# Attention and two feed-forward layers on one core: the first layer's up-projections from seven block products, and a fixed order for TensorE

## The chip, the cores and the metric
The kernel runs on one core of a Trainium2 chip. A core has TensorE (matmuls), VectorE, ScalarE and GpSimd, and SyncE (SP), whose queue starts nearly all transfers here. The metric is the device time of one execution in microseconds. Times of before and after come from several runs; durations of instructions come from one profiled execution each.

## The reference
```python
def phi(x):                                   # x: (4, 8, 576, 64), w_phi: (64, 128)
    proj = einsum('bhsd,df->bhsf', x, w_phi)
    proj = proj - max(abs(proj), axis=-1, keepdims=True)
    return concatenate([exp(proj), exp(-proj)], axis=-1)
q_p, k_p = phi(q), phi(k)
kv = einsum('bhsf,bhsd->bhfd', k_p, v);  z = sum(k_p, axis=2)
attn = einsum('bhsf,bhfd->bhsd', q_p, kv) / (einsum('bhsf,bhf->bhs', q_p, z)[..., None] + 1e-06)
x = attn.transpose(0, 2, 1, 3).reshape(2304, 512)
h = maximum(maximum(x @ w1, x @ w2), x @ w3)  # first layer, 512 -> 768
x = h @ w_out                                 # 768 -> 512
xn = x / sqrt(mean(x * x, -1) + 1e-06) * rms_g
g = xn @ w_gate                               # second layer, 512 -> 1536
out = (g / (1 + exp(-g)) * (xn @ w_val)) @ w_out2
```
All weights of the two layers are given as float64, all other inputs as float32.

## The kernel before
**Order.** The program collects operations in a `Planner`: each has an engine, a rank (its due time by hand-written formulas), an estimated duration, the buffers that it reads and writes and, on TensorE, a form ("rows": the array split in two by rows; "cols": split by columns; "whole"). `order` then places them one after the other by the estimated times, picks by rank among what could start within 0.11 us, gives every buffer a slot of its ring, and the program is written out in that order. So each engine's order is static, and a wait holds everything behind it on that engine. `SP` issues the loads, spills and fetches in one such order too.

**Attention.** Eight units (two heads of two batches each), each in three steps of 384 tokens. A step has, for TensorE, the projections of k (`k_proj`, L431, tile pk) and q (`q_proj`, L500, tile pq), the sums over tokens `kv_sum` (L464 and L461, tile pkv), `attend` (L531, tile nd) and `turn`, a transpose of the result (L551, tile pq). k_proj, q_proj and turn are in row form, kv_sum and attend in column form. Around them stand maxima, subtractions and exponentials on VectorE, ScalarE and GpSimd (an all-partition maximum for q). At the end of a step ScalarE rounds the transposed result (`x_round`, L559) and VectorE forms the remainder (`x_rest`, L562).

**Products in three parts.** Both operands of a matmul of the feed-forward layers are split into a rounded part and a remainder of TensorE's 32-bit format; a product is three matmuls, high x high, high x low, low x high (`mm3`, L386).

**Weights.** A weight tile of 512 columns is loaded in its double width (`wst`), and cut to single precision with five VectorE instructions (`narrow`, L657 to L671), then rounded by ScalarE (L679) and its remainder taken by GpSimd (L685, L687). The results go to 24 slots, `wp`.

**First layer.** For each of six blocks of 128 hidden features (m) and six tiles of 384 tokens (t): three up-projections of 12 matmuls each (`plan_up`, tiles first and up), their maximum (L871, L874), its split (L850, L851), and four down-projections of three matmuls (tile po), summed in `acc` by VectorE (L822). The first tiles of m = 0 (tile first) may run while attention ends.

**Second layer.** It works on token pairs (j) and pairs of hidden blocks already in seven block products instead of eight: `Duo` holds for one weight and a pair of tiles the sums "11", "12", "S1" to "S4", "22", `plan_forms` makes the matching block sums of the tokens, and `quad` issues for each weight the seven products of six matmuls into three accumulators (L1060, tiles ua and ub), from which ScalarE and VectorE (L1068, L1074, L1080, L1082) build the four results. Down-projections have 512 columns (tile pd). Token pairs 0 and 1 go through all six hidden pairs first; the weights are spilled to DRAM (`spill`) and come back (`fetch`) for token pair 2. The statistics for the norm (`plan_stats`, `plan_scale`) are taken at the end of the first layer.

## Time and profile before

| what | value |
|---|---|
| median of 3 runs | 868.77 us (867.83 to 869.34) |
| profiled execution | 867.84 us, its span 866.1 us |
| busy, share of the span | TensorE 98%, VectorE 75%, ScalarE 48%, GpSimd 26% |
| DMA | 98.68 MB, mean 114 GB/s |

The span goes from the first to the last instruction of the trace. A busy share is the union of an engine's instructions, each from its start to its end as the profiler records it; neighbouring instructions of one engine can overlap, so that their durations add to more than the time that they take. Ends of matmuls are modelled.

### The profile page before, as it was taken

Reading aid. Unit: us, or ns where it says so; the run is one execution under the profiler, and the core shown is the slowest. Engines: PE = TensorE matmul, PEld = TensorE weight load, DVE = VectorE, ACT = ScalarE, POOL = GpSimd, SP = SyncE. Lnnn points to the kernel's source line nnn. Section 1 sums busy time; section 2 is a strip of 40 time slices with the busy share of each in tenths; the row PEclk is TensorE's granted clock in tenths of the full one; section 3 lists DMA queues with packets and bytes.
Section 4 is the critical chain, followed back from the end, with each engine's and each line's share of the span. In section 5 each row is a group of like instructions: output and inputs, shape, how many; then the busy total and the mean of one; then the engine's idle time right before and its main releaser. Section 6 shows DMA issues by size and latency. Waiting matters only on the chain.

```text
span 866.1 us, 17038 instructions
## 1 busy us (share of the span) xinstructions
PE 853.0 (98%) x6784; PEld 801.3 (93%) x6784; DVE 650.8 (75%) x1301; ACT 413.0 (48%) x848; POOL 228.4 (26%) x157
## 2 busy tenths in 40 slices
PE   8999999999999999999998999999999999999997
PEld 7888889999999999999997999898989999999996
DVE  4899987888644986465998998998888867355445
ACT  5999994453211312124578755454535434432222
POOL 3555553454202311013244333322232200000000
PEclk9999999999999999999999999999999999999999
DMA  7444412132110123022012555544532213455551
GB/s 216 127 140 131 148 35 74 60 112 73 50 49 1 55 93 134 12 99 73 7 43 79 189 182 183 171 155 161 195 122 73 73 73 122 167 202 200 211 195 73
DMA packets 70686, 98.68 MB, mean 114 GB/s; under 512 B 5968, under 2 KB 42960, under 8 KB 70608
## 3 DMA queue, kind: packets, MB, share of 16 engines
q1 hardware_dynamic: 70528, 97.57, 33.7%
q8 instruction: 53, 0.87, 0.4%
q14 instruction: 25, 0.20, 0.1%
q10 hardware_dynamic: 80, 0.03, 0.0%
HBM read 69.27 MB, written 28.31 MB: 113 GB/s over the span
## 4 chain that ended last, share of the span: by engine, by line
PE 83%; DVE 9%; DMA 3%; ACT 3%; issue 1%; SPq 1%; POOL 0%; ACTq 0%; DVEq 0%
PE up L386 23%; PE pd L386 14%; PE ua L1060 13%; PE ub L1060 10%; PE po L386 8%; PE nd L531 4%; PE pkv L464 3%; DMA wst<-in_moe_w_gate_dram 2%; PE first L386 2%; PE pq L500 2%; PE pk L431 2%; DVE x L952 1%; DVE wm L671 1%; PE pq L551 1%; PE pkv L461 1%; DVE hl L851 1%
## 5 line engine op out<-in xcount | busy, mean ns | idle before, releaser
L386 PE MATMUL up<-x,wp 128*128 128x384 f32 x1188 | 216.9, 334 | 0.0
L386 PEld LDWEIGHTS up<-x,wp 128*128 128x128 f32 x1188 | 207.0, 188 | 0.0
L1060 PE MATMUL ua<-x,wp 128*128 128x384 f32 x720 | 142.0, 337 | 5.8 <-ACT sn L1068 2.4
L1060 PEld LDWEIGHTS ua<-x,wp 128*128 128x128 f32 x720 | 126.2, 188 | 10.9 <-ACT sn L1068 3.9
L386 PE MATMUL pd<-wp,hh 128*128 128x512 f32 x432 | 133.7, 390 | 0.0
L850 ACT CAST hh<-hf 128x384 fp32r<-128x384 f32 x108 | 55.1, 515 | 125.8 <-DVE hf L874 88.1
L1060 PE MATMUL ub<-x,wp 128*128 128x384 f32 x504 | 97.9, 335 | 0.3 <-DVE hf L1074 0.2
L386 PEld LDWEIGHTS pd<-wp,hh 128*128 128x128 f32 x432 | 80.6, 188 | 14.8
L685 POOL TENSOR_TENSOR wa<-wa,wp 128x512 f32<-128x512 f32 x32 | 45.0, 1405 | 177.2 <-ACT wp L679 121.7
L874 DVE TENSOR_TENSOR hf<-up,hf 128x384 f32<-128x384 f32 x66 | 36.7, 556 | 71.5 <-PE up L386 71.4
L1060 PEld LDWEIGHTS ub<-x,wp 128*128 128x128 f32 x504 | 88.4, 188 | 1.4 <-DVE hf L1074 0.5
L386 PE MATMUL po<-hh,wp 128*128 128x384 f32 x288 | 85.7, 337 | 0.2
L822 DVE TENSOR_TENSOR acc<-pd,acc 128x512 f32<-128x512 f32 x90 | 61.6, 687 | 32.3 <-PE pd L386 32.2
L386 PE MATMUL pd<-wp,hl 128*128 128x512 f32 x216 | 84.9, 393 | 0.0
L506 POOL PARTITION_ALL_REDUCE mq<-pc x24 | 66.5, 2779 | 56.6 <-ACT pc L503 51.4
L822 DVE TENSOR_TENSOR acc<-po,acc 128x384 f32<-128x384 f32 x120 | 64.4, 553 | 2.7 <-PE po L386 2.7
L851 DVE TENSOR_TENSOR hl<-hf,hh 128x384 fp32r<-128x384 f32 x108 | 62.8, 582 | 3.6 <-ACT hh L850 2.9
L1074 DVE TENSOR_TENSOR hf<-ub,hf 128x384 f32<-128x384 f32 x54 | 29.8, 553 | 42.0 <-ACT hf L1068 21.1
L650 ACT ACTIVATE wm<-wst 128x512 f32<-128x512 f32 x60 | 40.5, 675 | 39.3 <-DMA wst<-in_moe_w_gate_dram 16.3
L1068 ACT COPY sn<-ua 128x384 f32<-128x384 f32 x54 | 25.7, 477 | 65.4 <-PE ua L1060 65.3
L386 PEld LDWEIGHTS po<-hh,wp 128*128 128x128 f32 x288 | 53.0, 188 | 0.9 <-issue 0.4
L671 DVE SCALAR_TENSOR_TENSOR wm<-wst,wm 128x512 f32<-128x512 uint32 x60 | 49.8, 836 | 0.4
(102 smaller groups left out, 1448.4 us busy)
## 6 DMA issues: line engine op xcount, KB each, us to landing
wst<-in_moe_w_dram SPq DMA_DIRECT2D x18, 512.0 KB, 3.6
wst<-in_moe_w_out_dram SPq DMA_DIRECT2D x18, 512.0 KB, 3.6
wst<-in_moe_w_gate_dram SPq DMA_DIRECT2D x12, 512.0 KB, 4.1
wst<-in_moe_w_val_dram SPq DMA_DIRECT2D x12, 512.0 KB, 3.6
dwh<-wp SPq DMA_DIRECT2D x20, 256.0 KB, 2.8
wp<-dwh SPq DMA_DIRECT2D x20, 256.0 KB, 5.1
kraw<-in_kT_dram SPq DMA_DIRECT2D x24, 192.0 KB, 4.0
qraw<-in_qT_dram SPq DMA_DIRECT2D x24, 192.0 KB, 3.9
```

The lines of the kernel that those rows point to most:

```text
L386: mm(out=ps, lhsT=a, rhs=b, start=start and i == 0, stop=stop and i == n - 1)
L506: nc.gpsimd.partition_all_reduce(buf(f"mq{n}.{c}").rearrange("p a c -> p (a c)"), buf(f"pc{n}.{c}").rearrange("p a c -> p (a c)"), P, bass ...
L531: mm(out=nd[r, i, j * (D + 1):(j + 1) * (D + 1)], lhsT=e[:, j, q], rhs=kvs[:, u, b, :], start=u == 0, stop=u == 1)
L650: nc.scalar.activation(out=buf(f"wm{self.id}").bitcast(FP32), in_=self.view()[1].bitcast(FP32), func=ACTF.Abs)
L671: nc.vector.scalar_tensor_tensor(out=mf, in0=lo.bitcast(U32), scalar=2.0 ** -52, in1=mf, op0=ALU.mult, op1=ALU.mult)
L685: eng.tensor_tensor(out=a, in0=a, in1=r32(buf(self.h)), op=ALU.subtract)
L822: nc.vector.tensor_tensor(out=acc, in0=p, in1=acc, op=ALU.add)
L850: pl.op("ACT", rank, act_us(n), lambda: nc.scalar.copy(out=buf(h)[:, 0:n], in_=buf(f)[:, 0:n]), r=[f], w=[h])
L851: pl.op("DVE", rank + 0.6, dve_us(n), lambda: nc.vector.tensor_tensor(out=buf(l)[:, 0:n], in0=buf(f)[:, 0:n], in1=r32(buf(h)[:, 0:n]), op= ...
L874: pl.op("DVE", b_at(m, t, q), dve_us(n), lambda f=f, p=p, n=n: nc.vector.tensor_tensor(out=buf(f)[:, 0:n], in0=buf(p)[:, 0:n], in1=buf(f)[ ...
L1060: mm(out=buf(ps)[:, 0:TW], lhsT=x, rhs=y, start=start and n == 0, stop=stop and n == 3 * KH - 1, skip_group_check=True)
L1074: pl.op("DVE", q_at(i, q + off), dve_us(TW), lambda: nc.vector.tensor_tensor(out=buf(dst), in0=raw(), in1=buf(dst), op=ALU.add), r=[ps], w ...
```

## The change
The first layer gets the form of the second. Token pairs 0 and 1 go through all three pairs of hidden blocks (first pass), then token pair 2 (second pass); for each weight, `plan_chain` issues seven products of six matmuls. The new `Duo` of the first layer prepares pairs of weight tiles of w1, w2 and w3 (two of the nine pairs during attention, with VectorE taking their remainders), all weights of the first layer are spilled and come back for the second pass, and two hidden blocks share one accumulation of a down-projection. Attention's results are copied unsplit into `acc` (`x_out`, ScalarE); `plan_forms` makes the block sums of the tokens for both layers, each time with four differences and seven splits. The first chain has banks of its own ("fa", "fb") and may run while attention ends. In attention every operation of TensorE gets a place in one fixed line (`seq`): in each step attend of three steps ago and kv_sum (column form), then q_proj, k_proj of two steps ahead and turn (row form). The norm's statistics of token pairs 0 and 1 are planned into the second pass, and one pair of the second layer's weight tiles is prepared there ahead of its turn, spilled and fetched (`AHEAD`). Ring sizes, pools and many due times change with it.

```diff
+        line = sorted((o["seq"], o["i"]) for o in ops if o["seq"] is not None)
+        line = [i for _, i in line][::-1]
+
         def place(o):
-
...
+            if o["seq"] is not None and o["i"] != line[-1]:
+                return None
...
-    banks("up", (0, 1, 2, 3))
-    banks("first", (0, 1))
-    banks("po", (4, 5, 6, 7))
-    banks("pn", (7,))
+    banks("fa", (0,))
+    banks("fb", (1,))
     banks("ua", (0, 1))
     banks("ub", (2, 3, 4))
     banks("pd", (5, 6, 7))
+    banks("pn", (7,))
...
-    U = 17.65
-    LOAD = 0.4
+    U = 15.42
+    ORDER = (4, 5, 6)
+
+    def place_of(n, c, i):
+        return n * NCH + c, (ORDER.index(i) + 4 if i > 3 else i)
+
+    def at_step(n, c, i):
+        a, b = place_of(n, c, i)
+        return U / 3 * (a + 0.14 * b)
+
+    LEAD, QLEAD, TLAG = 2, 3, 0
...
-            pl.op("PE", rk - 9.34, KPROJ, lambda c=c: k_proj(c), r=["wphi", f"kraw{n}.{c}"], w=pk, form="rows")
+            pl.op("PE", at_step(n, c - LEAD, 5), KPROJ, lambda c=c: k_proj(c), r=["wphi", f"kraw{n}.{c}"], w=pk + ["klast"] * (n == NU - 1 and c == NCH - 1), form="rows", seq=place_of(n, c - LEAD, 5))
...
+                pl.op("PE", at_step(n, c, 2 + j), (NSUB + (c == 1)) * 2 * HALF, lambda c=c, j=j: kv_sum(c, j), form="cols", seq=place_of(n, c, 2 + j),
...
-        def x_round(c, h, t, a0, a1, b0, b1):
-            nc.scalar.copy(out=x_at("h", t, hp)[:, b0:b1], in_=buf(f"xt{n}.{c}.{h}")[:, a0:a1])
-
-        def x_rest(c, h, t, a0, a1, b0, b1):
-            nc.vector.tensor_tensor(
-                out=x_at("l", t, hp)[:, b0:b1], in0=buf(f"xt{n}.{c}.{h}")[:, a0:a1], in1=r32(x_at("h", t, hp)[:, b0:b1]),
-                op=ALU.subtract,
-            )
+        def x_out(c, h):
+            a = hp * TW + h * CH
+            dst, src = buf(f"raw{g * NCH + c}")[:, a:a + CH], buf(f"xt{n}.{c}.{h}")[:, 0:CH]
+            if XENG[h] == "ACT":
+                nc.scalar.copy(out=dst, in_=src)
+            else:
...
+            pl.op("PE", at_step(n, c + 3 - QLEAD, 4), 0.65, lambda c=c: q_proj(c), form="rows", r=["wphi", qr], w=pq, seq=place_of(n, c + 3 - QLEAD, 4))
...
+                pl.op("PE", at_step(n, c + 3, j), 6 * HALF, lambda c=c, j=j: attend(c, j), form="cols", seq=place_of(n, c + 3, j),
...
+            pl.op("PE", at_step(n, c + 3 + TLAG, 6), 0.16, lambda c=c: turn(c), form="rows", r=["ident", xs], w=xt, seq=place_of(n, c + 3 + TLAG, 6))
+            for h in range(2):
+                raw = new(f"acc{g * NCH + c}", f"raw{g * NCH + c}")
+                pl.op(XENG[h], rk + 5.37, act_us(CH, True) if XENG[h] == "ACT" else dve_us(CH), lambda c=c, h=h: x_out(c, h), r=[xt[h]], w=[f"{raw}:{hp}.{h}"])
...
-            eng = nc.vector if self.id < 4 else nc.gpsimd
+            eng = nc.gpsimd
...
+            e = self.early
+            last, gate = [] if e else ["mqlast"], [] if e == 2 else ["kdone"]
+            veng = "DVE" if e else VENG
+            reng = ["DVE"] * 4 if e else RENG
...
+    VENG = "DVE"
+    RENG = ["POOL", "POOL", "POOL", "DVE"]
+    duos1 = [[Duo(w, m, max(0, 2 - i) if m == 0 else 0) for i, w in enumerate((w1, w2, w3))] for m in range(NM1)]
+    rows1 = [[rows(wo1, 2 * m + z) for z in range(2)] for m in range(NM1)]
+    duos2 = [[Duo(w, m) for w in (wg, wv)] for m in range(NM2)]
+    rows2 = [[rows(wo2, 2 * m + z) for z in range(2)] for m in range(NM2)]
...
-    def plan_up(rank, key, piece, t, ring="up"):
-        ps = new(ring, f"up{key}")
-
-        def fn():
-            wh, wl = buf(piece.h), buf(piece.l)
-            mm3(buf(ps)[:, 0:TW], [(wh[:, k * P:(k + 1) * P], wl[:, k * P:(k + 1) * P], x_at("h", t, k), x_at("l", t, k)) for k in range(KD)])
-
-        pl.op("PE", rank, 12 * mm_us(TW), fn, r=xin(t) + [piece.h, piece.l], w=[ps], lag=0.2, when=EARLY)
-        return ps
...
+    PROD = 6 * mm_us(TW)
+    CHAIN = 7 * PROD
+    DOWN2 = 6 * R512
+    XM = 6 * CHAIN + 16 * PROD
+    YM = 3 * CHAIN + 8 * PROD
+    GQ = 2 * CHAIN + 2 * TW // P * DOWN2
+    Y0 = A + NM1 * XM
+    F0 = Y0 + NM1 * YM
+    FB = F0 + 2 * NM2 * GQ
...
+    CHAINS = [[(u, j) for j in range(2) for u in range(3)]] + [[(u, j) for u in range(3) for j in range(2)]] * (NM1 - 1)
+    for m in range(NM1):
+        step = XM / 8
+        r0 = A + XM * (m - 1) + 16.84
+        for i in range(3):
+            duo = duos1[m][i]
+            if m:
+                r = (r0 + 2 * i * step, r0 + (2 * i + 1) * step)
+            elif i < 2:
+                r = (41.2 + 24.41 * 2 * i, 41.2 + 24.41 * (2 * i + 1))
+            else:
+                r = (A - 12.5, A - 12.5 + 5.0)
+            duo.plan(r, A + XM * m + CHAIN * CHAINS[m].index((i, 0)))
+            for n in duo.slots:
+                spill(n, r[1] + SPL)
+        for z in range(2):
+            r = r0 + (6 + z) * step if m else A - 12.5 + 10.0 + 5.0 * z
+            rows1[m][z].plan(r, A + XM * m + 6 * CHAIN)
+            for n in (rows1[m][z].h, rows1[m][z].l):
+                spill(n, r + SPL)
+
+    def names(duos, rws, m, tag=""):
+        return [[n + tag for n in d.slots] for d in duos[m]] + [[n + tag for p in rws[m] for n in (p.h, p.l)]]
...
+    for m in range(NM1):
+        for i, k in enumerate(names(duos1, rows1, m)):
+            for x, n in enumerate(k):
+                fetch(n, Y0 + YM * m + CHAIN * i - 14.89 + 0.5 * x, Y0 + YM * m + CHAIN * i + 0.01 * x)
+    LAST = NM2 - 1
+    AHEAD = [(1, 0)]
...
+            if (m, i) in AHEAD:
+                r = [Y0 + 6.66 + 7.0 * (2 * AHEAD.index((m, i)) + z) for z in range(2)]
+                duos2[m][i].plan(r, r[1] + 8.0)
+                for x, n in enumerate(duos2[m][i].slots):
+                    spill(n, r[1] + SPL)
+                    fetch(n, need - 29.02 + 0.5 * x, need + 0.01 * x, ".p")
+                continue
...
+        split(0.0, "11", b11)
+        mix(0.7, b11, b12, b11)
+        split(1.2, "T1", b11)
+        mix(1.9, b12, b22, b12)
+        split(3.0, "T3", b12)
+        mix(2.0, b11, b22, b11)
+        split(2.2, "T2", b11)
+        split(0.5, "21", b21)
+        mix(3.5, b21, b21, b11)
+        split(4.0, "T4", b21)
+        split(4.5, "22", b22)
...
+    def plan_chain(layer, key, u, duo, ws, j, r0, hfring, gate, rings=("ua", "ub"), when=0.0):
+        f = {}
+        a, b, c = new(rings[0], f"a{key}.{u}"), new(rings[1], f"b{key}.{u}"), new(rings[1], f"c{key}.{u}")
+        final = u == (2 if layer == 1 else 1)
+
+        def product(q, ps, wf, xf, start):
+            def fn():
+                n = 0
+                for k in range(KH):
+                    wh, wl = duo.forms(ws, wf, k)
+                    xh, xl = (buf(f"f{i}{layer}.{j}.{xf}")[:, k] for i in "hl")
+                    for x, y in ((wh, xh), (wh, xl), (wl, xh)):
+                        mm(out=buf(ps)[:, 0:TW], lhsT=x, rhs=y, start=start and n == 0, stop=n == 3 * KH - 1, skip_group_check=True)
+                        n += 1
+            w = ([ws[6]] if ws[6][-2:] in (".b", ".p") else [ws[6] + ":h", ws[6] + ":l"]) if wf == "22" else [
+                n for h, p in zip(HALVES, ((ws[0], ws[1]), (ws[2], ws[3]), (ws[4], ws[5]))) if wf in h for n in p]
+            pl.op("PE", r0 + q, PROD, fn, r=w + [f"f{h}{layer}.{j}.{xf}:{k}" for h in "hl" for k in range(KH)] + ["klast"] * (when > 0.0), w=[ps], lag=0.2, when=when)
+
...
+        def result(q, zt, ps, sole=False):
+            hf = f"hf{key}.{zt}"
+            dst = f"v{key}.{u}.{zt}" if u else hf
+            raw, fin = of(ps), of(ps if sole else dst)
+            if not sole:
+                pl.op("DVE", r0 + q, dve_us(TW), lambda: nc.vector.tensor_tensor(out=buf(dst), in0=raw(), in1=buf(dst), op=ALU.add), r=[ps], w=[dst])
...
+            elif u:
+                pl.op("DVE", r0 + q + 0.7, dve_us(TW), lambda: nc.vector.tensor_tensor(
+                    out=buf(hf), in0=fin(), in1=buf(hf), op=ALU.mult if layer == 2 else ALU.max), r=[ps], w=[hf], lock=0.0 if sole else dve_us(TW))
...
+        product(0.0, a, "11", "11", True)
+        copy(1.1 * x, "00")
+        product(1.04 * x, b, "12", "21", True)
+        result(2.2 * x, "00", b)
+        product(2.1 * x, a, "S2", "T2", False)
+        copy(3.2 * x, "01")
+        product(3.1 * x, c, "S1", "T1", True)
+        product(5.2 * x, a, "S3", "T3", False)
+        copy(6.3 * x, "11")
+        result(6.8 * x, "11", c)
+        product(8.0 * x, a, "22", "T4", False)
+        result(9.1 * x, "10", a, True)
+        product(9.1 * x, c, "S4", "22", False)
+        result(10.2 * x, "01", c)
...
+                def down(ps=ps, hid=hid, k=k):
                     s = slice(k * P, (k + 1) * P)
-                    mm3(buf(ps)[:, 0:n], [(buf(wo.h)[:, s], buf(wo.l)[:, s], buf(h)[:, 0:n], buf(l)[:, 0:n])])
...
-    for i, (m, j, tag) in enumerate(plan):
-        quad(i, m, j, tag)
+            plan_forms(1, j, k, 104.92 + 5.3 * k if j == 0 else A - 4.81 + 5.3 * k)
+    for m in range(NM1):
+        nm = names(duos1, rows1, m)
+        f = [None, None]
+        for i, (u, j) in enumerate(CHAINS[m]):
+            first = m == 0 and i == 0
+            f[j] = plan_chain(1, f"1.{m}.{j}", u, duos1[m][u], nm[u], j, A + XM * m + CHAIN * i, "hfx",
+                              [] if first else ["kdone"], ("fa", "fb") if first else ("ua", "ub"), EARLY if first else 0.0)
+        for j in range(2):
+            plan_down1(f"1.{m}.{j}", f[j], nm[3], j, A + XM * m + 6 * CHAIN + 8 * PROD * j, m == 0)
+    for k in range(KH):
+        plan_forms(1, 2, k, Y0 - 20.0 + 5.3 * k)
+    for m in range(NM1):
+        nm = names(duos1, rows1, m, ".b")
+        for u in range(3):
+            f = plan_chain(1, f"1.{m}.2", u, duos1[m][u], nm[u], 2, Y0 + YM * m + CHAIN * u, "hf", [])
+        plan_down1(f"1.{m}.2", f, nm[3], 2, Y0 + YM * m + 3 * CHAIN, m == 0)
+    N0 = Y0 + 1.89
+    for t in range(4):
...
+    late = F0 + 11.21 * GQ
+    for t in (4, 5):
+        plan_stats(t, F0 + 19.51 + 6.0 * (t - 4), 8.16)
...
+    order = [(m, j, "") for m in range(NM2) for j in range(2)] + [(m, 2, ".b" if m < LAST else "") for m in range(LAST, -1, -1)]
+    for i, (m, j, tag) in enumerate(order):
+        nm = names(duos2, rows2, m, tag)
+        for u in range(2):
+            if j < 2 and (m, u) in AHEAD:
+                nm[u] = [n + ".p" for n in nm[u]]
+            f = plan_chain(2, f"2.{i}", u, duos2[m][u], nm[u], j, F0 + GQ * i + 3.3 * u, "hf", [])
+        first = i < 2 or i == 2 * NM2
+        plan_down2(f"2.{i}", f, nm[2], j, F0 + GQ * (i + 1), first, i in (2 * NM2 - 2, 2 * NM2 - 1, 3 * NM2 - 1))
 
```

## Rows read from the trace of the kernel before

**Rows 1.** Busy by stretch: length, PE, PEld, DVE, ACT, POOL us (instructions), clock, DMA share, GB/s
```profile
40.00:100.00 60.00, 59.50 (x1399) 52.30 (x1396) 56.32 (x133) 57.16 (x131) 33.11 (x12) 1.00 0.51 151
165.00:400.00 235.00, 235.00 (x1358) 235.00 (x1357) 163.88 (x313) 64.02 (x123) 57.06 (x42) 1.00 0.21 69
407.00:480.00 73.00, 69.22 (x387) 64.35 (x385) 65.43 (x135) 52.31 (x103) 25.73 (x20) 1.00 0.12 42
480.00:660.00 180.00, 177.93 (x931) 165.09 (x930) 162.94 (x327) 89.53 (x179) 54.55 (x40) 1.00 0.49 165
```

**Rows 2.** The chain of waits, first and second layer: start us, us, what
```profile
157.21 4.16 PE up L386 x24
...
165.53 4.16 PE up L386 x24
...
557.59 6.84 PE pd L386 x30
```

**Rows 3.** Tiles of the early up-projections and of the turns, TensorE
```profile
L386 PE MATMUL first<-x,wp x108: 334/334/446, 124.6 to 155.3; 128*128 128x384 f32 x108
...
L551 PE MATMUL pq<-ident,xs x144: 212/223/275, 25.5 to 144.3; 64*128 64x64 f32 x144
```

**Rows 4.** TensorE in order of time, attention: start us, us, what
```profile
60.66 0.92 PE L464 MATMUL pkv<-vt,e 128*64 128x65 f32 x24
61.51 0.40 PE L551 MATMUL pq<-ident,xs 64*128 64x64 f32 x6
61.84 0.34 PE L531 MATMUL nd<-kvs,eq 128*64 128x65 f32 x4
...
63.39 0.92 PE L500 MATMUL pq<-qraw,wst 64*128 64x384 f32 x4
...
65.24 2.32 PE L464 MATMUL pkv<-vt,e 128*64 128x65 f32 x72
...
68.89 0.92 PE L500 MATMUL pq<-qraw,wst 64*128 64x384 f32 x4
```

**Rows 5.** VectorE by line, 40 to 100 us: count, busy us, mean ns, idle before, releaser
```profile
L562 DVE TENSOR_TENSOR x<-pq,x 128x192 fp32r<-128x192 f32 x24 | 7.4, 350 | 1.6 <-ACT x L559 1.5
```

**Rows 6.** VectorE in order of time, start of the second layer
```profile
463.67 0.55 DVE L1082 TENSOR_TENSOR hf<-ua,hf 128x384 f32<-128x384 f32 x1
464.14 0.55 DVE L1074 TENSOR_TENSOR sn<-ub,sn 128x384 f32<-128x384 f32 x1
...
467.58 0.68 DVE L671 SCALAR_TENSOR_TENSOR wm<-wst,wm 128x512 f32<-128x512 uint32 x1
```

**Rows 7.** VectorE by line, 165 to 405 us, cutting of weight tiles
```profile
L671 DVE SCALAR_TENSOR_TENSOR wm<-wst,wm 128x512 f32<-128x512 uint32 x23 | 19.6, 865 | 0.3
...
L665 DVE SCALAR_TENSOR_TENSOR wa<-wst,wm 128x512 int32<-128x512 int32 x23 | 16.4, 729 | 0.2
L657 DVE TENSOR_SCALAR wm<-wm 128x512 f32<-128x512 f32 x23 | 12.1, 543 | 2.9 <-ACT wm L650 2.8
L669 DVE TENSOR_SCALAR wm<-wa 128x512 int32<-128x512 int32 x23 | 11.2, 502 | 0.1
L661 DVE TENSOR_SCALAR wm<-wm 128x512 int32<-128x512 int32 x23 | 10.4, 469 | 0.2
```

**Rows 8.** Busy time from 780 to 790 us, columns as in rows 1
```profile
780.00:790.00 10.00, 10.00 (x56) 9.53 (x55) 5.91 (x11) 3.80 (x8) 0.00 (x0) 1.00 1.04 381
```

**Rows 9.** Busy time of four tiles (pd, ua, ub, po) from 432.00 to 564.44 us
```profile
432.00:564.44 132.44, 41.04 (x174) 32.55 (x174) 10.93 (x16) 7.08 (x12) 1.00 0.41 141
...
432.00:564.44 132.44, 50.39 (x253) 44.18 (x254) 2.75 (x5) 17.39 (x37) 1.00 0.41 141
...
432.00:564.44 132.44, 37.88 (x192) 33.60 (x192) 16.84 (x31) 1.00 0.41 141
...
432.00:564.44 132.44, 4.83 (x24) 1.00 0.41 141
```

**Rows 10.** Waits of SP's queue, longest in total: us, times, longest us
```profile
SPq L639 <- DVE wm L671: 303.8, 47, 49.0
```

More of the change, by code (lines that the diff above doesn't have):

```diff
@@ L39 @@
 NTT = NT // TW
-CW = (TW,) * NTT
-C0 = tuple(TW * t for t in range(NTT))
-WIDE = TW
-NPAIR = NTT // 2
+NM1 = N1 // 2
 NM2 = N2 // 2
@@ L117, in order @@
         freed = {b: 0.0 for b in touch}
+        for o in ops:
+            o["todo"] = sorted(o["bufs"], key=turn.get)
         free, start, end = {}, {}, {}
-        ready, dma_free, seq, kind = {}, 0.0, [], "plain"
+        ready, dma_free, loads, seq, kind = {}, 0.0, 0, [], "plain"
         cand, form, held = {}, None, {"DVE": (-1.0, -1.0, -1.0), "POOL": (-1.0, -1.0, -1.0)}
@@ L720, in rows, with __init__, engine @@
         return Piece(w[m * P:(m + 1) * P, :], 1)
-    pieces1 = [[columns(w, m) for w in (w1, w2, w3)] + [rows(wo1, m)] for m in range(N1)]
     HALVES = ("11", "12"), ("S1", "S2"), ("S3", "S4")
     class Duo:
-        def __init__(self, w, m):
+        def __init__(self, w, m, early=0):
+            self.early = early
             self.p = [columns(w, 2 * m + z) for z in range(2)]
             self.slots = [f"{self.p[0].h}.{n}" for n in ("1h", "1l", "Ah", "Al", "Bh", "Bl", "22")]
+        def engine(self, name):
+            return nc.gpsimd if name == "POOL" and not self.early else nc.vector
         def forms(self, names, form, k):
```

510 lines of the change are left out of this document (201 added, 309 removed).

## The prediction
> **What bounds the kernel now.** I read the page's shares first (the table above), then the busy times by stretch, the chain of waits, the order of TensorE's instructions in attention, and the groups on VectorE. TensorE's and VectorE's shares of the span are means over three stages with different limits, so the stretches count [rows 1]. In attention (40 to 100 us) three engines are near their limit at once: TensorE 59.5 of 60, ScalarE 57.2, VectorE 56.3. In the first feed-forward layer (165 to 400 us) TensorE alone is full, 235 of 235, and VectorE stands at 163.9, 70%. Where the second layer begins (407 to 480 us) TensorE idles 3.8 of 73 us with VectorE at 90%; further into it (480 to 660 us) VectorE is again at 90%, and TensorE loses 2.1 of 180. The granted clock is 1.00 in each, so matmuls of one size have one price throughout. So this is a TensorE kernel; whatever takes matmuls away pays in full, until VectorE stands where TensorE stood.
>
> The price of a matmul comes from the chain of waits [rows 2]: 24 with 384 columns last 4.16 us, 0.1733 us each, and one token tile of the first layer, 48 of them, goes from 157.21 to 165.53, 8.32 us, the same price with nothing lost. With 512 columns, 30 take 6.84 us, 0.228 each.
>
> **Matmuls removed.** Before, the up-projections take 36 matmuls for each of six f-blocks and six token tiles, 1,296; the tile of the early ones has its 108 of them in [rows 3]. After, one chain is seven products of six matmuls, 42, for two f-blocks, two token tiles and one weight: 3 x 3 x 3 chains, 1,134. The down-projections stay at 432 (72 groups of six instead of 144 of three). 162 matmuls fewer x 0.1733 = **-28.1 us** on the engine that sets the time.
>
> **Attention's order.** One step before [rows 4]: 24 kv matmuls take 60.66 to 61.51, 0.85 us; the turn 0.33; attend with 48 matmuls 1.55, to 63.39. Where kv and attend stand in one run, 72 and 48 matmuls take 65.24 to 68.89, 3.65. By the first step alone they would cost 2.40 plus 48 kv matmuls; at attend's own slope, (1.55 - 0.15)/48 = 0.029, these are 1.40, so a joint run saves 0.15 us. The turn stands alone between two column runs in 18 of the 20 steps up to 124.5 us, as it does at 61.51. 24 steps with two changes save 18 to 24 times 0.15, 2.7 to 3.6: **-3**. [...]
>
> It can be less, since ScalarE has 2.8 us of slack in 60 [rows 1], which are 12 steps (two subtractions each) [rows 5]: 0.23 in each 5 us, hardly more than a step would gain; and one order of seven groups makes everything behind a late group wait. So the bounds are -4 and 0 here, and more as a rival. VectorE is relieved: 24 subtractions of 350 ns (of 48 in all) leave this stretch [rows 5], since the transposed blocks are now only copied. Their work comes back later as block forms. At the end of attention, before, the gaps hold the early up-projections from 124.6 us on, the last turn starting at 144.3 [rows 3]. After, one chain of 42 matmuls, 7.3 us, and the first three products of the next, 3.1 us, can fill these gaps; the rest waits for banks that the last turns hold. What is left in the last three steps (three attends, three turns) is 5.6 us of work in some 15 us, so 10.4 us of filler is just enough. I cost that at nothing; without the cover it is up to 5 us.
>
> **VectorE in the first token pass.** Here the change can give its gain back. The spacing of VectorE's 384-column instructions is 0.47 us (463.67 to 464.14) though each is shown as 0.55 [rows 6]: neighbours overlap by 0.08. Cutting one weight tile out of its double-width source is five instructions, in the first layer 865 + 729 + 543 + 502 + 469 ns = 3.11 us [rows 7], less five overlaps 2.7. First pass (two token pairs, three f-pairs, six blocks):
> Results: 3 + 7 + 7 for the three chains and 4 remainders, 21 a block, 126; sums of the down-projections 8 in four of the blocks (ScalarE does the first pair's), 32. 158 x 0.47 = 74 us.
> Weights: seven pairs of tiles and six single ones are still to cut when the pass starts (two pairs are done in attention): 20 x 2.7 = 54; two totals, four sums and one remainder a pair, 7 x 7 x 0.47 = 23.
> Block forms for the second and third token pair: 2 x 2 x (4 + 7) = 44 x 0.47 = 21.
> That is 172 us. TensorE's part is 1,044 matmuls, 180.9 us, less the chain that went ahead, 173.6. VectorE is at 99% of TensorE: the cover of the old first layer (30% slack) is gone. At 90% TensorE lost 1.2% in the settled second layer and 5.2% at its start [rows 1]. For 99% I take the higher, **+9 us**; bounds are 2 us (1.2%) and, with every instruction at its full shown duration (158 x 0.55 + 20 x 3.11 + 93 x 0.55 = 200), +26. What is late then is a result: a chain's accumulators stay occupied in their banks and TensorE stops ahead of the next chain's first product.
>
> **Third token pair, second pass.** 522 matmuls, 90.5 us. VectorE: 63 results and 16 sums, 37 us; eight tiles of the second layer's weights with three pairs' sums, 22 + 10; the second layer's forms and scales, some 17: 86 us, 95%. **+3**, bounds 1 and 8. New here is DMA: 75 weight tiles of 256 KB that were sent out in the first pass come back, 19.7 MB, with eight loads of 512 KB, 4.2 MB, and some sixteen spills, 4.2 MB, 28 MB in 90 us, 310 GB/s. The trace has moved 381 GB/s over 10 us while TensorE stayed full [rows 8], so it fits, with little to spare. I cost it at nothing; its price is under the rivals.
>
> **Start of the second layer.** Between 432.00 and 564.44 us TensorE did 174 matmuls of 512 columns, 253 and 192 of the two product kinds and 24 late down-projections [rows 9]: 39.7 + 469 x 0.1733 = 121.0 us, with at most 5 for the small ones of the statistics; 6 to 11 of 132.4 us were lost. After the change four of six token tiles have their statistics in the second pass and one pair of weights is ready ahead of time. I take **-5**, bounds 0 and -9.
>
> **Sum.** 866.1 - 28.1 - 3 + 9 + 3 - 5 = 842.0 us of span; the profiled execution lies 1.7 above its span, and the median of the runs 0.9 above that, 844.6: **845 us**.
>
> **Rivals.**
> *VectorE sets the first pass.* GpSimd does 33 remainders in it (three for each pair of tiles, two for each single one), at 57.06/42 = 1.36 us each [rows 1]. One instruction of the tile cutting takes 0.68 us undisturbed (467.58) [rows 6] but 865 ns on average where GpSimd is subtracting beside it [rows 7]: VectorE is held. If each GpSimd instruction holds it for half its length, 22 us are added to 172, 194 against 173.6, +20 in place of +9; with 5 in place of 3 later, 858. [...]
> *VectorE is covered.* The planner interleaves well, and waits stay at 2 and 1: 836 us.
> *The fixed order loses.* If every step waits 0.3 us for ScalarE, which works 95% of this stretch, 24 steps give +7 in place of -3: 855.
> *Slower than before: the refetches stand behind loads.* All transfers leave through SP in one order. Its 47 loads of weights that waited for VectorE's last cutting step waited 303.8 us in all, 6.5 each, up to 49 [rows 10]; nothing urgent stood behind them before. In the second pass eight such loads stand among the 75 refetches, with a lead of 15 us. Eight waits of 6.5 are 52, less the lead 37 us of TensorE: 882. It decides from 5 us a wait. Against it: few loads are due at a time when VectorE has caught up.
>
> **How the numbers follow.** Forecast 0.45 (by itself 839 to 852), VectorE bound 0.20, covered 0.15, fixed order 0.11, refetches behind loads 0.09. The range 830 to 862 leaves out the last, half of what exceeds the full-duration bound, and the combinations of all lower ends. Runs of this kernel differ by 0.2%, so less than that counts as same. The first four cases are faster nearly throughout: faster 0.89, same 0.03, slower 0.08.
>
> **What would show it.** Right: 1,134 up-matmuls, two changes of form a step and steps of some 4.85 us, the first layer's matmuls over by some 410 us, VectorE over 93% busy in the first pass and TensorE idle there by 4 to 6%. Wrong: TensorE idle over 15 us in the first pass with results or block forms as releaser (VectorE bound), attention's last turn later than 144 us (fixed order), TensorE waiting for fetched tiles in the second pass (refetches), or a lower granted clock anywhere, which no term allows for.

## The result and the profile after

The changed kernel takes 857.63 us (median of four runs, 855.30 to 858.70), the kernel before 868.3 beside it: ratio 0.9874, 95% interval 0.9849 to 0.9898. So 10.7 us were gained where 23.8 had been forecast. The profiled execution has a span of 855.5 us, against 866.1.

From the page of the changed kernel: busy time, share of the span and instructions; the granted clock in 40 slices; the chain that ended last.

```profile
PE 830.9 (97%) x6622; PEld 778.3 (91%) x6622; DVE 696.2 (81%) x1389; ACT 451.5 (53%) x958; POOL 219.0 (26%) x150
...
PEclk9999999999999999899998999999999999999999
...
PE 78%; DVE 14%; ACT 3%; issue 2%; DMA 1%; POOL 1%; SPq 0%; DVEq 0%; ACTq 0%; POOLq 0%
```

TensorE's busy time fell by 22.1 us (853.0 before, the page's share in the table of before), and its idle time, span less busy, rose from 13.1 to 24.6. Two dents in the clock are new, in slices 17 and 22. Busy by stretch, columns as in [rows 1], first the changed kernel:

```profile
0.00:40.00 40.00, 34.12 (x664) 30.29 (x666) 25.90 (x56) 30.35 (x66) 18.32 (x21) 1.00 0.67 194
40.00:126.00 86.00, 85.67 (x2018) 76.13 (x2014) 80.25 (x178) 85.37 (x201) 47.19 (x18) 1.00 0.43 132
126.00:180.00 54.00, 48.02 (x401) 43.50 (x396) 51.36 (x108) 30.68 (x69) 14.43 (x9) 1.00 0.41 143
180.00:340.00 160.00, 158.71 (x908) 156.15 (x907) 145.24 (x290) 74.30 (x156) 47.12 (x35) 1.00 0.53 180
340.00:384.00 44.00, 40.50 (x211) 39.23 (x211) 35.12 (x71) 22.02 (x52) 6.79 (x7) 0.88 0.67 224
384.00:438.00 54.00, 54.00 (x309) 53.06 (x308) 44.41 (x91) 26.13 (x53) 12.98 (x10) 1.00 0.65 225
438.00:458.00 20.00, 16.16 (x84) 15.53 (x83) 19.70 (x34) 11.51 (x25) 8.05 (x7) 0.83 0.43 146
458.00:660.00 202.00, 202.00 (x1057) 187.77 (x1057) 184.05 (x363) 105.93 (x206) 58.84 (x43) 1.00 0.45 153
```

and the kernel before, over attention and the start of its second layer:

```profile
0.00:40.00 40.00, 37.58 (x694) 32.11 (x694) 25.37 (x59) 29.89 (x66) 15.95 (x20) 1.00 0.54 161
40.00:126.00 86.00, 85.50 (x1939) 74.33 (x1937) 79.10 (x184) 82.18 (x185) 48.59 (x18) 1.00 0.42 125
126.00:180.00 54.00, 54.00 (x479) 51.66 (x478) 42.11 (x82) 28.40 (x62) 22.11 (x15) 1.00 0.22 69
406.00:490.00 84.00, 80.00 (x448) 74.80 (x447) 75.93 (x156) 60.23 (x120) 31.75 (x23) 1.00 0.20 70
```

Four stretches lose time: 5.9 us of idle TensorE in the first 40 us (2.4 before), 6.0 from 126 to 180, where attention ends (none before), 3.5 from 340 to 384, where the second token pass begins, with the clock at 0.88, and 3.8 from 438 to 458, where the second layer begins, with the clock at 0.83. The long stretches between lose little: in the first pass (180 to 340) TensorE idles 1.3 us, and its 908 matmuls at 0.1733 us make 157.4 of the 160, with VectorE at 91%; from 384 to 438 and 458 to 660 TensorE is full.

The waits at these places. TensorE in order of time, end of attention (the step that waits longest) and begin of the second pass:

```profile
148.43 0.34 PE L983 MATMUL ua<-xAT4h,wp 128*128 128x384 f32 x1
150.44 0.44 PE L983 MATMUL ub<-xA22h,wp 128*128 128x384 f32 x1 [1.67 <-DVE sn L1001]
...
152.75 0.40 PE L567 MATMUL pq<-ident,xs 64*128 64x64 f32 x6
...
154.23 0.33 PE L983 MATMUL ub<-xAT1h,wp 128*128 128x384 f32 x1
...
346.85 0.44 PE L983 MATMUL ua<-xAT3h,wp 128*128 128x384 f32 x1 [0.89 <-ACT sn L994]
...
349.04 0.62 PE L983 MATMUL ua<-xAT4h,wp 128*128 128x384 f32 x1 [0.86 <-ACT sn L994]
349.45 0.52 PE L983 MATMUL ua<-xAT4l,wp 128*128 128x384 f32 x1
349.77 0.84 PE L983 MATMUL ua<-xAT4h,wp 128*128 128x384 f32 x2
...
450.53 0.69 PE L983 MATMUL ua<-xA11l,wp 128*128 128x384 f32 x1 [3.84 <-DVE xA11l L953]
```

ScalarE's copy ahead of the first of these waits (first line), VectorE behind it, and VectorE where the second layer begins:

```profile
144.64 0.48 ACT L994 COPY sn<-ua 128x384 f32<-128x384 f32 x1 [1.42 <-PE ua L983]
...
146.84 0.68 DVE L754 TENSOR_TENSOR wa<-wa,wm 128x512 f32<-128x512 f32 x1
...
147.56 0.42 DVE L767 TENSOR_TENSOR wm<-wa 128x256 f32<-128x256 f32 x1
147.90 0.55 DVE L558 TENSOR_TENSOR xs<-nd,den 128x384 f32<-128x384 f32 x1
148.36 0.41 DVE L767 TENSOR_TENSOR wm<-wm,wa 128x256 f32<-128x256 f32 x1
148.70 0.42 DVE L767 TENSOR_TENSOR wm<-wa 128x256 f32<-128x256 f32 x1
149.03 0.55 DVE L1001 TENSOR_TENSOR hfx<-fb,hfx 128x384 f32<-128x384 f32 x1
149.50 0.42 DVE L767 TENSOR_TENSOR wm<-wa,wm 128x256 f32<-128x256 f32 x1
149.83 0.55 DVE L1001 TENSOR_TENSOR sn<-ub,sn 128x384 f32<-128x384 f32 x1
...
448.19 0.55 DVE L953 TENSOR_TENSOR xAT4l<-acc,xAT4h 128x384 fp32r<-128x384 f32 x1
448.65 1.35 DVE L953 TENSOR_TENSOR xA22l<-acc,xA22h 128x384 fp32r<-128x384 f32 x1
449.93 0.55 DVE L953 TENSOR_TENSOR xA11l<-acc,xA11h 128x384 fp32r<-128x384 f32 x1
```

The reader is to see three things. At 149.83 comes the result that TensorE waits for (sn). The copy to which it adds was done at 145.12; in between VectorE makes, among others, the sums of the third pair of weight tiles (L754, L767), whose first use as a sum is the product S1 x T1 at 154.23. At 349.04 the first matmul after the second wait lasts 0.62 us, and from 349.45 on matmuls start 0.32 us apart (0.17 in [rows 2]): the granted clock is 0.50 from 349.5 to 354 us, and 1.00 from 340 to 349. And at 449.93 the remainder of the first block form, xA11l, the one TensorE needs next, comes after those of the later forms T4 and 22; TensorE waited 3.84 us for it.

The theory to be tested: not the settled passes but the three places where one set of block forms gives way to the next lose the time, since there only the three chains of one token pair are left and their results stand in VectorE's and ScalarE's queues among work that isn't urgent; the clock that fell in or behind such waits (0.88 from 340 to 384 us, 0.83 from 438 to 458) adds to it. Rivals: the fixed order of attention costs; VectorE's total work costs, wherever it stands.

### The profile page after: what moved, and what is told of

It reads as the page before. It is cut to its first block, busy times and chain, and to the rows that moved or that the text cites. A ratio compares the mean times of both kernels' runs of the same rounds, so it can differ in the third digit from the quotient of the medians.

```text
span 855.5 us, 17220 instructions
## 1 busy us (share of the span) xinstructions
PE 830.9 (97%) x6622; PEld 778.3 (91%) x6622; DVE 696.2 (81%) x1389; ACT 451.5 (53%) x958; POOL 219.0 (26%) x150
## 4 chain that ended last, share of the span: by engine, by line
PE 78%; DVE 14%; ACT 3%; issue 2%; DMA 1%; POOL 1%; SPq 0%; DVEq 0%; ACTq 0%; POOLq 0%
PE ua L983 24%; PE pd L394 23%; PE ub L983 18%; PE nd L547 4%; PE pkv L480 3%; PE pq L516 2%; PE pk L447 2%; DVE hfx L1009 2%; DVE sn L1001 1%; DVE wa L671 1%; DVE wm L677 1%; DVE acc L946 1%; PE pq L567 1%; DVE hl L1015 1%; PE pkv L477 1%
## 5 line engine op out<-in xcount | busy, mean ns | idle before, releaser
L839 DVE TENSOR_TENSOR acc<-pd,acc 128x512 f32<-128x512 f32 (+1 forms) x138 | 87.8, 642 | 55.7 <-PE pd L394 55.3
L1001 DVE TENSOR_TENSOR sn<-ub,sn 128x384 f32<-128x384 f32 x108 | 59.3, 554 | 49.4 <-PE ub L983 27.0
L781 POOL TENSOR_TENSOR wp<-wm,wp 128x512 fp32r<-128x512 f32 x38 | 52.2, 1392 | 99.7 <-ACT wp L778 53.3
L394 PE MATMUL pd<-hh,wp 128*128 128x384 f32 x288 | 77.2, 338 | 0.3 <-DVE acc L839 0.3
L1014 ACT CAST hh<-hf 128x384 fp32r<-128x384 f32 x84 | 42.5, 513 | 35.6 <-DVE hf L1009 35.1
L394 PEld LDWEIGHTS pd<-hh,wp 128*128 128x128 f32 x288 | 53.0, 190 | 0.6 <-DVE acc L839 0.6
L466 ACT ACTIVATE e<-e 128x384 f32<-128x384 f32 x96 | 47.3, 557 | 8.0 <-DVE e L459 7.8
L394 PEld LDWEIGHTS pd<-wp,hl 128*128 128x128 f32 x216 | 40.5, 187 | 8.9 <-DVE hl L1015 0.4
L394 PE MATMUL pd<-hl,wp 128*128 128x384 f32 x144 | 48.5, 337 | 0.0
L671 DVE SCALAR_TENSOR_TENSOR wa<-wst,wm 128x512 int32<-128x512 int32 x60 | 44.4, 740 | 0.1
L1009 DVE TENSOR_TENSOR hf<-sn,hf 128x384 f32<-128x384 f32 x72 | 43.6, 607 | 0.4
```

The lines of the kernel that those rows point to most:

```text
L394: mm(out=ps, lhsT=a, rhs=b, start=start and i == 0, stop=stop and i == n - 1)
L466: nc.scalar.activation(out=dst, in_=src, func=ACTF.Exp, scale=-1.0 if u else 1.0)
L671: nc.vector.scalar_tensor_tensor(out=ai, in0=hi, scalar=-0x40000000, in1=m, op0=ALU.bitwise_and, op1=ALU.bitwise_or)
L781: self.engine(RENG[i]).tensor_tensor(out=self.dest(i, 1), in0=self.source(i), in1=r32(self.dest(i, 0)), op=ALU.subtract)
L839: nc.vector.tensor_tensor(out=acc, in0=p, in1=acc, op=ALU.add)
L1001: pl.op("DVE", r0 + q, dve_us(TW), lambda: nc.vector.tensor_tensor(out=buf(dst), in0=raw(), in1=buf(dst), op=ALU.add), r=[ps], w=[dst])
```

## The experiments

All times are medians beside runs of the kernel before on the same chip (867.8 to 869.0); the changed kernel's ratio is 0.9874 (0.9849 to 0.9898), and gains and losses "by the ratio" are differences from it, times 868 us. Versions that leave work out compute something else; they tell only what that work costs.

**Less cutting at the end of attention.** In the cutting, `if self.light and step != 2: return`, light for five tiles.

> The changed kernel with four of the five cutting steps left out for the five weight tiles of the first block that are cut between 126 and 180 us (the second tile of the second weight, both of the third, both of the output weight); 20 VectorE instructions, about 11 us of its work, the order of all others as it was. Theory (VectorE, full from 126 to 180 us, holds the end of attention): TensorE's loss between 126 and 180 us falls from 9.3 us to 3 to 5, the last transpose comes 3 to 5 us sooner than 152.9, the time is 4 to 6 us shorter (852 to 854). Rival (the fixed order of TensorE holds the end of attention): the loss stays at 8 to 9.3 us and the time within 1.5 us of 857.6.

Measured: 855.14, ratio 0.9859 (0.9843 to 0.9875). VectorE fell from 51.36 to 45.71 us of 54 and TensorE idled 4.6 us there instead of 6.0. So about a quarter of this loss is the cutting; the time is 1.3 us shorter by the ratio, which can't be told from none, and neither the theory (852 to 854) nor the rival's unchanged loss came out. The other 4.6 us stay. In the changed kernel 2.6 of the 6.0 us wait for ScalarE's copies of a chain's accumulator, 2.0 for VectorE's results and 0.7 for a block form. This version kept the sums of the weight tiles (L754, L767), and the wait for sn was still 1.44 us (1.67 before); whether these sums hold it was not tried.

**No statistics for the first four blocks.** All of the statistics and scaling of t = 0 to 3 replaced by nothing.

> The changed kernel with the squares, sums, roots and scaling of the first four token blocks left out. Theory (these stand in ScalarE's, VectorE's and TensorE's queues ahead of the second pass's first results, and the waits bring the clock down): TensorE loses at most 2 us of the 8 between 340 and 384 us, the granted clock stays at 1.00 there, the time is 6 to 8 us shorter (850 to 852). Rival (the refetched tiles, 270 to 340 GB/s there, or the second pass's own first chain): the clock still falls, 5 us or more stay lost, the time within 3 us of 857.6.

Measured: 844.68, ratio 0.9740 (0.9728 to 0.9753), 11.6 us by the ratio; more than forecast. The clock is 1.00 from 340 to 384 us, and TensorE does 243 matmuls there, 211 before, of which 27 were short ones of the statistics. The refetched tiles still come (297 GB/s there), so the rival that they hold this stretch is out.

**No mixing of the second pair's forms.** `lambda: (layer, j) != (2, 1) and ...` around the subtraction.

> The changed kernel with the eight subtractions left out that mix the blocks of the second layer's second token pair (4.1 and 2.2 us of VectorE between 438 and 458 us). Theory (VectorE, 19.9 of 20 us busy there, is late with these forms): the wait of 3.84 us at 450.5 falls to under 1, the clock stays at 1.00, the time is 3 to 6 us shorter (852 to 855). Rival (the wait comes from ScalarE's parts of the forms or from the first chain's results): the wait stays above 2.5 us, the time within 1.5 us of 857.6.

Measured: 855.28, ratio 0.9880 (0.9854 to 0.9906); the wait for xA11l is 2.7 us. Nothing that can be told from no change: eight instructions fewer on a full VectorE don't help while the urgent one stands last.

**The three together.**

> The three together. Theory (three separate losses): they add up, 14 to 18 us shorter than the changed kernel (840 to 844). Rival (one engine's total work sets the whole, and a wait taken away comes back later): less than two thirds of the sum of the three single gains, 847 or more.

Measured: 844.61, ratio 0.9731 (0.9719 to 0.9744), hardly more than without the statistics alone. Neither the theory's range (840 to 844) nor the rival's (847 or more) was met. By the ratios the single gains are 1.3, 11.6 and -0.5 us, and the three together 12.4, which is their sum; but two of them can't be told from nothing, so this run doesn't tell whether the losses are separate.

**The fixed order, taken away and tried alone.** In the one, `seq=None` for every operation; in the other, only `line`, `place_of`, `at_step` and the ranks of attention put into the kernel before.

> The changed kernel with TensorE's order in attention left to the planner again; all else as it was. Theory (two changes of form a step save what the sum said): steps of 5.0 us in place of 4.87 between 45 and 120 us, the end of attention 2 to 4 us later, the time 2 to 4 us longer (859 to 862). Rival (the line itself costs, at the start, where TensorE idles 5.9 us in the first 40 against 2.4 in the kernel before, and at the end): TensorE idles under 3.5 us in the first 40 us and the time is 2 us or more shorter (under 856).

> The kernel before with the fixed line alone (its ranks and step length too); the first layer stays at 36 matmuls a tile and the transposed blocks are rounded where they were. Theory (the term of the sum, -3 us): 863.5 to 866.5 against 868. Rival (three engines are full in attention, so the changes of form were covered, or late groups hold all behind them): 867.5 or more.

Measured: 863.35 without it, ratio 0.9939 (0.9920 to 0.9958); alone in the kernel before 869.49, ratio 1.0005 (0.9993 to 1.0018). Starts of attend 14 steps apart, before, with the line in before, and after:

```profile
46.13 0.29 PE L531 MATMUL nd<-kvs,eq 128*64 128x65 f32 x4
...
118.83 0.34 PE L531 MATMUL nd<-kvs,eq 128*64 128x65 f32 x4
```

```profile
48.00 0.34 PE L548 MATMUL nd<-kvs,eq 128*64 128x65 f32 x4
...
118.78 0.34 PE L548 MATMUL nd<-kvs,eq 128*64 128x65 f32 x4
```

```profile
47.65 0.34 PE L547 MATMUL nd<-kvs,eq 128*64 128x65 f32 x4
...
117.43 0.34 PE L547 MATMUL nd<-kvs,eq 128*64 128x65 f32 x4
```

Steps of 5.19, 5.06 and 4.98 us. In the kernel before the fixed order shortens the steps by about 0.13 (1.9 us in 14), and loses as much as all steps gain by a slower start: TensorE is busy 34.10 of the first 40 us with it, 37.58 without. In the changed kernel it is worth 5.7 us, more than the 2 to 4 expected, and hardly through the steps: without it the last attend comes sooner (135.4 us against 146.3), but the last turn later (156.1 against 152.9), and so do the early chains (first product 127.3 us against 121.7, first down-projection 187.1 against 178.5); TensorE idles 8.8 us from 126 to 180 with the clock at 0.83 from 160 to 180. The slow start is the line's (37.22 busy of 40 without it, 34.12 with it), but on the whole the rival that it costs is out.

**Statistics further apart.** `plan_stats(t, Y0 + 14.0 + 10.0 * t, 8.0)`, with scaling and forms later; then two versions between.

> The changed kernel with the same work; the statistics of the first four token blocks are ranked 10 us apart from 14 us into the second pass on (they were 5 apart from 2 on), their sums on TensorE 8 us later against their squares, scaling and first forms 25 to 35 us later. Theory (the 6 us that leaving them out gave beyond their own work on TensorE came from their place in the queues): the clock stays at 1.00 from 340 to 384 us and the time is 3 to 6 us shorter (852 to 855). Rival (the work itself is what costs, wherever it stands): within 1.5 us of 857.6; or it is only moved into the start of the second layer: longer.

> As stats_spread, but the scaling and forms of the first pair follow as soon as its statistics are there (ranked 35 us into the second pass, forms from 36), those of the second pair at 55. Spreading left VectorE busy 9.2 of 24 us from 360 to 384 and full from 390 to 410. Theory (place in the queues, not work): nothing lost from 340 to 384 us as there, and less than the 9.8 us that it lost from 384 to 458; 851 to 855. Rival (VectorE's total up to the second layer is too much, the loss only moves): 856 to 859.

> As the changed kernel, with the four statistics ranked 7 us apart from 10 us into the pass (5 from 2 before), sums 6 us later, scaling at 24 and 42. Theory: between the two, the first loss mostly gone, little moved; 852 to 856. Rival: 856 to 859.

Measured: 858.40, ratio 0.9877 (0.9860 to 0.9893); 867.45, ratio 0.9982 (0.9966 to 0.9999); 860.80, ratio 0.9912 (0.9884 to 0.9940). The first, by stretch:

```profile
340.00:384.00 44.00, 43.24 (x257) 42.86 (x256) 25.17 (x48) 20.54 (x46) 9.46 (x9) 1.00 0.83 286
384.00:438.00 54.00, 50.01 (x273) 48.65 (x273) 50.73 (x108) 28.94 (x60) 11.79 (x9) 0.94 0.44 155
438.00:458.00 20.00, 14.22 (x75) 13.92 (x74) 19.36 (x33) 11.96 (x25) 9.42 (x8) 0.83 0.44 147
```

From 340 to 384 us TensorE does 236 matmuls of chains and down-projections where it did 182, 54 more, 9.4 us at 0.1733; from 384 to 458, where VectorE now has 70.1 of 74 us, it does 319 where it did 379, 10.4 us less. All of the loss moved. The two versions between are slower than the changed kernel, by 9.4 and 3.3 us by the ratio. So none of three other places gave anything back; the rival (the work, wherever it stands) holds as far as these go.

**Which part of the statistics.** No scaling (`t > 3 and ...` ahead of it); one square of four, and no sums on GpSimd; and, beside them, 32 cutting steps of the second layer left out.

> The changed kernel without the 16 VectorE instructions that scale the first four blocks (some 9 us of VectorE between 355 and 372 us); squares, sums, roots and transposes stay. If VectorE's queue is what costs: 4 to 8 us shorter than the changed kernel (850 to 854), the clock falls less from 340 to 384. If ScalarE's and GpSimd's part costs: within 1.5 us of 857.6.

> The changed kernel with three of four squares left out for each of the first four blocks (12 ScalarE instructions, some 5 us) and GpSimd's 12 sums (13 us); everything behind them stays. If ScalarE's queue is what holds the chains' copies (the waits of 0.9 us for sn at 346 to 349 us, after which the clock falls): 4 to 8 us shorter (850 to 854), the clock 1.00 from 340 to 360. If VectorE's scaling costs: within 1.5 us.

> The changed kernel with four of five cutting steps left out for the eight weight tiles of the second layer that are cut in the second pass and at the second layer's start (32 VectorE instructions, some 17 us); statistics as they were. If VectorE's total from 330 to 460 us is what costs: 6 us or more shorter (under 852). If only the place of the statistics in the queues costs: the 8 us from 340 to 384 stay, and the time is at most 3 us shorter, from the second layer's start.

Measured: 852.19, ratio 0.9811 (0.9778 to 0.9843); 853.23, 0.9832 (0.9803 to 0.9862); 851.49, 0.9823 (0.9784 to 0.9861). By the ratios these are 5.5, 3.6 and 4.4 us below the changed kernel, only the first by an interval clear of its own. Each median lies in the range of its own theory, so these theories don't exclude each other. They touch different engines, and the first two, with some 3.5 us of TensorE for the sums and transposes (four times 0.72 and 0.49 us as shown, less overlaps), come to 12.6 where leaving all out gave 11.6 by the ratio. No single queue is the cause, as far as these intervals tell; it is a stretch in which ScalarE, GpSimd, VectorE and TensorE hand each block's work on. VectorE is not full in all of it: 13.3 of 20 us from 340 to 360, 21.8 of 24 from 360 to 384. The runs of one version lie wide apart, and their mean granted clocks with them:

```
no scaling:            849.66 (0.998)  850.40 (0.997)  853.97 (0.992)  855.78 (0.990)
second cutting light:  849.58 (0.998)  851.19 (0.995)  851.79 (0.996)  857.02 (0.990)
changed kernel:        855.30 (0.993)  857.21 (0.989)  858.05 (0.990)  858.70 (0.992)
```

In the first two a clock lower by 0.008 goes with 6.1 and 7.4 us.

**The second pair's forms sooner.** Rank 19 us sooner; then only the second half moved up, 1.0 us behind the first (5.3 before); then 0.5 and both 2 us sooner: `n0 + 5.0 + 5.3 * k if j == 0 else F0 + 5.17 + 0.5 * k`.

> The changed kernel with the block forms of the second layer's second token pair ranked 19 us sooner and the two halves 1 us apart (they were 5.3); nothing left out. Theory (at 445.7 to 451.5 us TensorE waits for one remainder of the first form, xA11l, which stands in VectorE's queue behind nine forms and sums that are needed later; leaving out the mixes only moved it by 1.1 us): the wait of 3.84 us falls under 1.5, the clock stays at 1.00, the time is 3 to 5 us shorter (853 to 855). Rival (VectorE is full there and another wait follows): within 1.5 us of 857.6.

> The changed kernel with only the rank of the second half of the second pair's forms (second layer) moved: 1.0 us after the first half, 5.3 before. Moving all 19 us sooner put them ahead of the last results of the second pass (a wait of 6.1 us for hf). Theory (xA11l of the second half is late only because forms of the first half that are needed later stand ahead of it): the wait of 3.84 us falls under 2, 854 to 856. Rival (VectorE is full from 438 to 458 us, another wait takes its place): 857 or more.

> As halves_close (854.8), the two halves 0.5 us apart and both 2 us sooner. Theory (the urgent form's remainder comes sooner): 852 to 855. Rival (as for forms 19 us sooner, chain results fall behind): 857 or more.

Measured: 865.97, ratio 0.9958 (0.9940 to 0.9975), with a wait of 6.1 us for a chain's result (hf L1009); 854.83, 0.9840 (0.9823 to 0.9857); 853.66, 0.9839 (0.9819 to 0.9859). In the last:

```profile
438.00:458.00 20.00, 18.48 (x107) 17.42 (x107) 19.04 (x37) 13.46 (x27) 9.08 (x6) 1.00 0.43 146
```

```profile
441.73 0.55 DVE L953 TENSOR_TENSOR xA11l<-acc,xA11h 128x384 fp32r<-128x384 f32 x1
```

xA11l is done 8 us sooner, the wait of 3.84 us is gone (the longest left there is 0.90), the clock stays at 1.00, with the same work and VectorE still at 95%. At this place it was order, not load: the theory holds for the wait, and the time is 3.0 us shorter by the ratio in both, though either interval still touches the changed kernel's. Moving everything sooner failed, and shows that the chain results are the other urgent ones.

**Do the waits bring the clock down?** Both as the last version. One product of the second pass's first block done twice ahead of the wait at 346 us, and four matmuls nobody reads ahead of the sums; then no added work, but the last down-projections of the first pass ranked at half pace (`rank = r0 + gap * PROD * (KD * x + k)`, gap 2).

> As halves_nearer (853.7, clock 0.83 and 0.93 from 340 to 384 us), with one product of the second pass's first block done twice just ahead of the wait of 0.88 us at 346 us, and four matmuls of 128 columns ahead of the sums at 351 us whose result nobody reads; 10 matmuls more, some 1.5 us of TensorE. If the waits bring the clock down: the clock stays at 1.00 from 340 to 384 us in most runs, and the time is 1 to 4 us shorter in spite of the added work (850 to 853). If the clock falls for another reason: as before there, and 0 to 2 us longer.

> As halves_nearer, with the sixteen-group down-projection that ends the first pass ranked at half its pace, so that half of its groups stand between the products of the second pass's first block; no work added or left out. Theory (the block has three chains and nothing else to do while their copies are made): TensorE waits under 1 us from 344 to 353, the clock stays at 1.00, 848 to 852. Rival (the statistics of the last two blocks come later by it and hold the second layer's forms): 853 or more.

Measured: 855.43, ratio 0.9836 (0.9819 to 0.9854), and 853.33, 0.9818 (0.9801 to 0.9834). The first, TensorE's stretches and its waits in order of time:

```profile
350.00:360.00 10.00, 9.14 (x58) 8.78 (x58) 7.05 (x11) 4.47 (x11) 3.37 (x3) 1.00 0.93 333
360.00:370.00 10.00, 6.63 (x32) 6.22 (x31) 7.88 (x19) 4.38 (x11) 0.00 (x0) 0.83 0.62 222
```

```profile
352.08 0.45 PE L983 MATMUL ua<-xAT4h,wp 128*128 128x384 f32 x1 [0.85 <-ACT sn L996]
...
363.15 0.80 PE L1102 MATMUL pn<-ones,tm 128*128 128x1 f32 x6 [2.62 <-DVE acc L1118]
```

From 350 to 360 us the clock was 0.70 in the changed kernel (first line below); with one of the two waits for sn filled it is 1.00, and falls only after a later wait of 2.62 us. That alone would say that the waits bring it down. But in the profiled execution of halves_close both waits stand unfilled, and the clock is 1.00 as well:

```profile
350.00:360.00 10.00, 9.76 (x43) 9.40 (x42) 7.72 (x16) 3.35 (x8) 3.05 (x3) 0.70 0.79 268
```

```profile
347.46 0.44 PE L983 MATMUL ua<-xAT3h,wp 128*128 128x384 f32 x1 [0.89 <-ACT sn L994]
...
349.65 0.44 PE L983 MATMUL ua<-xAT4h,wp 128*128 128x384 f32 x1 [0.86 <-ACT sn L994]
```

```profile
350.00:360.00 10.00, 7.36 (x47) 7.03 (x45) 10.00 (x19) 4.06 (x10) 3.38 (x3) 1.00 0.96 325
```

Of the eight profiled executions that have both waits unfilled, the clock fell behind them in three (the changed kernel, no scaling, halves_nearer). So that filling them kept the clock up is not shown. What the comparison does show is that the dip is paid in part by time in which TensorE would wait anyway: in halves_close it idles 5.1 us from 340 to 384 with the clock at 0.92, among it 2.64 us for the scaling that VectorE has not finished; in the changed kernel it idles 3.5 us with the clock at 0.88. The expectation of 1 to 4 us failed, as the ratio is that of halves_nearer. The second version failed its theory too (848 to 852, waits under 1 us): the clock stays at 1.00 until 352 us, but TensorE waits 1.1 and 2.1 us. It is the fastest of those that leave nothing out, by an interval that doesn't touch the changed kernel's, though not to be told from halves_nearer.

## Why the prediction was right and wrong

Direction and range held, the size did not: the span came out 13.5 us above the sum of 842.0. Term by term:

- **Matmuls, -28.1:** right. The page counts 162 matmuls fewer, and a product of six takes 1.04 us in the first pass.
- **Attention's order, -3:** each step is shorter by 0.13 us, as said, though 4.98 and not 4.85 long. But alone it is worth 0 (from 0.6 us shorter to 1.6 longer): the slow start, 3.5 us of idle, was not in the sum. The sign named for a fixed order that loses, a last turn later than 144 us, was seen (152.9), but without the line it is 156.1.
- **End of attention, costed at nothing:** the step that failed first. I counted 10.4 us of filler as just enough and named 5 us without the cover; 6.0 us are idle. The filler was there in amount, but it is chains that wait for their own results and copies, beside a VectorE with 51.4 of 54 us.
- **VectorE in the first pass, +9:** it came out as 2.6 (1.3 us idle, the rest in matmuls that start late behind waits). I put 172 us of VectorE there. Of the 20 tiles five are cut from 126 to 180 us and 15 behind it (beside them one of an early pair, and two of the second layer), and the 22 instructions of the second pair's forms stand there too: some 13 + 10 us of the 172 had moved ahead, into the very stretch that I costed at nothing. The last cutting step in the two stretches:

```profile
L677 DVE SCALAR_TENSOR_TENSOR wm<-wst,wm 128x512 f32<-128x512 uint32 x6 | 5.6, 931 | 0.0
```

```profile
L677 DVE SCALAR_TENSOR_TENSOR wm<-wst,wm 128x512 f32<-128x512 uint32 x17 | 13.5, 794 | 0.0
```

- **Second pass, +3, bounds 1 and 8:** some 8.5, all of it in its first 44 us (3.5 idle, and by estimate up to 5.3 for a clock of 0.88 over 44 us), the rest full. I averaged 86 us of VectorE over 90, 95%. At the start, where the first four blocks' statistics stand, it has 35.1 of 44 us, 80%; it is the handing on of single blocks that costs, and leaving the statistics out gave 11.6 us. The refetches, the rival that was to make it slower, cost nothing: 302 GB/s at its start and no wait of TensorE on a transfer.
- **Start of the second layer, -5:** about 0. Idle 3.8 us and by estimate up to 3.4 for the clock (0.83 over 20 us) stand against 3.8 and 2.1 before [rows 1]. Work done ahead didn't help where the order of two halves of one form held TensorE: 3 us came back with it.

Sum: 866.1 - 28.1 + 6.0 + 2.6 + 8.5 = 855.1, beside a span of 855.5; the terms are not known so well that the closeness means much. That the sum of 842.0 isn't further off is luck: the +9, too high by 6, hid a part of the other misses. The common error is one: VectorE's load was summed over long passes, and compared with TensorE's sum, where the trace of before already lost its time at beginnings [rows 1]. No term allowed for the clock, which the text named as what would make it wrong; its mean is 0.989 against 1.00. One sign did not fit the sum itself: the first layer's last down-projection starts at 450.3 us before, from which -28.1 - 3 + 9 + 3 make 431, not 410; it came at 438.5. What stays open: how the 8.5 us of the second pass split between clock and wait, since one takes the other's place from run to run; what brings the clock down there; and the 4.6 us at the end of attention that remain without the cutting: a version with other work ready there, or with the chain results ahead of the sums, was not tried.

## What to carry to other kernels

Cost a change that removes matmuls stretch by stretch, and look hardest at the places where one set of operands gives way to the next: there the chains have only each other to hide behind, and an average of VectorE's load says nothing. When a wait names one instruction on a full engine, look at what stands ahead of it and is needed later, before taking work away: moving one half of the forms by 4.3 us in rank gave 3 us, and leaving eight instructions out gave none. And where a loss stays or grows wherever the same work is placed (here the statistics, at three other places), ranks don't mend it; leaving out a part of that work did.
